# Four heads of the first input: three hardware-queue loads become five, one head each

## The chip, the cores and the metric

The kernel runs on one core of a Trainium2 chip. The metric is the device time of one execution in microseconds (us); lower is better. Times are given as the median of several executions; one further execution is recorded by the hardware profiler, and all lines of the profile come from that one.

A core has five engines that run at the same time, each with its own instruction queue: TensorE (PE, matrix products; PEld is its loading of weights), VectorE (DVE), ScalarE (ACT), GpSimd (POOL) and SyncE (SP). They wait for one another through semaphores only. Data between the main memory and the core's memory is moved by 16 DMA engines. A transfer is issued from the instruction queue of SyncE, ScalarE or POOL, and its packets then appear in the profile under that issuer's DMA queue: q1 for SyncE, q10 for ScalarE, q0 for POOL.

## The reference: what is computed

Cross attention between a long input x (8 batches, 8 heads, 512 rows, 64 columns) and a short state (32 rows), in both directions, and then a gated feed-forward layer on all 4352 rows of the result:

```python
scores = scale * np.matmul(x, state.transpose(0, 1, 3, 2))
a = np.exp(scores - scores.max(-1, keepdims=True))
xread = np.matmul(a / a.sum(-1, keepdims=True), state)
scores2 = scale * np.matmul(state, x.transpose(0, 1, 3, 2))
a2 = np.exp(scores2 - scores2.max(-1, keepdims=True))
sread = np.matmul(a2 / a2.sum(-1, keepdims=True), x)
y = concatenate([xread, sread], axis=2), heads side by side: (4352, 512)
out = (np.maximum(y @ w_gate, 0.0) * (y @ w_val)) @ w_out
```

w_gate and w_val are 512 x 1536, w_out is 1536 x 512; inputs and output are float32.

## The kernel before

Everything is computed in bf16 with float32 sums. For each batch the state's rows are multiplied with the gate and value weights first (U, in PSUM as `up` or `upc`), so that the gate and value of the long rows are one product of the normalised attention weights (`ans`) with U (`gv_ps`, line 325). ReLU runs on ScalarE (line 354), the product with the value on VectorE (line 358), the product with w_out on TensorE (`o_ps`, line 367), and the result leaves through SyncE's queue (line 379).

The order of every engine's instructions is written out by hand: the schedule is manual (line 412), and a program string (lines 455 to 483) lists the steps of the first two batches and part of the third in the order in which they are issued. A step is a name with numbers, and `@` gives the PSUM banks. Each engine takes its own instructions strictly in that order and waits where the data is not there yet. From line 525 on, loops issue the rest with fixed positions.

The steps that matter here are those of the first microseconds, for batch 0:

- Lines 414 to 420 load the state of batches 0 and 1 (`st_f`, 128 KB, `state_dma`, line 99) and heads 0 to 3 of batch 0 (`xf`, float32, 128 KB a head). SyncE issues heads 0 and 1 as one transfer, ScalarE the state and then heads 2 and 3 as one transfer. ScalarE then runs a one-element exp (line 421), which loads its table.
- Line 427 loads heads 4 to 7 of batch 0 from POOL, with the cast to bf16 on the way (`xb`). POOL goes on with batch 1 (`dx`, line 434) and then the weights (`dw`, line 109), in pieces.
- `spin32.2` and `spin` (line 440) are TensorE fillers whose result (`warm_ps`) is not used. The first fills TensorE until the state is there.
- `stc.0` casts the state on VectorE (line 118), `stT.0` transposes it on TensorE (line 123), `sto.0.0` and `sto.0.1` copy it out, on ScalarE and VectorE (line 140).
- `xc.0.0` casts heads 0 and 1 to bf16 on ScalarE, `xc.0.1` heads 2 and 3 on VectorE (both line 144).
- `xT.0.0.4` and `xT.0.4.4` transpose these pairs on TensorE (line 162), `xo` copies the transposes out (line 165): the first on VectorE, the second on ScalarE.
- `sc.0.0` computes the scores of heads 0 to 3 (line 179), `ex` their exp on ScalarE (line 206), `nr` the sums on VectorE (lines 212, 214), `nx` the scaling (line 218), and `aT`/`ao` transpose the weights into `ans`. Steps of batch 0's other heads and of batch 1 are woven in. The first `c` steps make U (line 298), and `gv.0.0` is the first product of the dense part.

The program's words around the change, of which TensorE, VectorE and ScalarE each take their own:

```python
xc.0.0.act spin.1.256 xT.0.0.4@1 xc.0.1.dve sto.0.0.act
spin.1.128 xT.0.4.4@2 xo.0.0.4.dve sto.0.1.dve xo.0.4.4.act spin.1 sc.0.0@3 ex.0.0 nr.0.0 spin.1.384
    xT.0.8.4@4 xT.0.12.4@5 xo.0.8.4.act xo.0.12.4.act spin.1 xT.1.0.8@6 sc.0.1@1 ex.0.1 xo.1.0.8.dve spin.1
```

So VectorE's queue holds, in this order, the cast of heads 2 and 3, the copy of the first transposes, and the copy of half the state; the scores wait for all of them.

Of the kernel before, what the change touches and what calls it, by code (L numbers as in the profile page):

```python
# [16 lines left out]
def kernel(  # L17
# [9 lines left out]
    nc = tc.nc  # L27
# [6 lines left out]
    NC = S // 128  # L34
# [43 lines left out]
    xf, xb, xT, eT, e_sn, a_sn, ANS, U, hsb = {}, {}, {}, {}, {}, {}, {}, {}, {}  # L78
# [18 lines left out]
    def state_dma(eng, lo, hi):  # L97
        src = state.rearrange("(g b) h (m i) d -> (b h m) g i d", b=2, i=4)
        eng.dma_start(out=st_f[:, lo // 2:hi // 2], in_=src[:, lo // 2:hi // 2])
# [312 lines left out]
    ctx.enter_context(tc.manual_schedule())  # L412
    nc.vector.memset(stT, 0.0)
    xf[0] = xin.tile([128, HK, NC, D], FP32, name="xf", tag="xf")
    for eng, j in ((nc.sync, 0), (nc.scalar, None), (nc.scalar, 1)):
        if j is None:
            state_dma(eng, 0, 2)
        else:
            src = x[0, 2 * j:2 * j + 2].rearrange("h (p c) d -> p h c d", c=NC)
            eng.dma_start(out=xf[0][:, 2 * j:2 * j + 2], in_=src)  # L420
    nc.scalar.activation(out=tiny, in_=nc.const_aps.tensor(0.0, (128, 1), FP32), func=AF.Exp)

    def w_load(w, lo, n):
# [179 lines left out]
```

## Time and profile before

| What | Value |
|---|---|
| Median of 3 executions | 220.07 us (219.66 to 220.4) |
| The profiled execution | 219.39 us |
| Its span, first to last instruction | 217.6 us |
| Issue to landing: state, ScalarE's queue, 128 KB | 2.6 us |
| Issue to landing: heads 0 and 1, SyncE's queue, 256 KB | 3.3 us |
| Issue to landing: heads 2 and 3, ScalarE's queue, 256 KB | 3.5 us |
| Issue to landing: heads 4 to 7 and batch 1's halves, POOL's queue, 256 KB each | 5.3 us (median of 3) |
| Granted TensorE clock | 1.00 in all slices |

The span is what the engines' instructions cover; the 1.8 us between it and the profiled execution's time lie around them. In lines of the timeline the first number is the start in us from the span's start, the second the length; then come the engine, the line of the kernel, the operation, what it writes and reads, and in brackets the idle time before it and what ended it. An engine name with a q (SPq, ACTq) is the issue of a transfer on that engine's queue. In the chain of waits a line is a piece of the chain that ended last: start, length, engine, tile and line.

### The profile page before, as it was taken

The page shows a single profiled execution, that of the slowest core. Times are in us where ns is not written, and L with a number is a line of the kernel's source. Part 1 is how long each engine was busy: PE and PEld are TensorE (multiplying, and loading weights), DVE is VectorE, ACT ScalarE, POOL GpSimd, SP SyncE. Part 2 cuts the span into 40 slices and gives each one's busy share as a digit, 9 for nine tenths or more (in the row PEclk, how much of TensorE's full clock was granted, in tenths as well). Part 3 has the DMA queues.
Part 4 walks back from the last instruction along what each step waited for, and adds up shares of the span by engine and source line. Part 5 has one row for each costly group of instructions (what it writes and reads, how often), then busy time and mean ns, then how long its engine had stood idle before and what let it go on. Part 6 is the DMA issues. An engine that isn't in the chain of part 4 may idle for free.

```text
span 217.6 us, 4865 instructions
## 1 busy us (share of the span) xinstructions
PE 212.8 (98%) x1952; PEld 104.8 (48%) x1952; DVE 135.0 (62%) x233; ACT 117.8 (54%) x225; POOL 42.5 (20%) x63
## 2 busy tenths in 40 slices
PE   8899999999999999999999999999999999999994
PEld 4554454454444444444444444444544445666543
DVE  4799967956887678557966796388745444222100
ACT  4798877747546556455555656454646443333221
POOL 7974049005600531020107000000000000000000
PEclk9999999999999999999999999999999999999999
DMA  7999999579963995919491453131311122222132
GB/s 168 180 196 197 202 221 171 78 139 188 152 175 74 144 186 110 167 52 193 99 148 60 110 134 96 49 99 50 84 28 51 48 48 50 61 56 80 51 96 96
DMA packets 47399, 24.96 MB, mean 115 GB/s; under 512 B 27824, under 2 KB 43056, under 8 KB 47376
## 3 DMA queue, kind: packets, MB, share of 16 engines
q0 software_dynamic: 16896, 9.05, 31.0%
q1 hardware_dynamic: 29584, 14.85, 28.7%
q10 hardware_dynamic: 896, 0.75, 1.3%
q8 instruction: 15, 0.25, 0.4%
q14 instruction: 8, 0.07, 0.2%
HBM read 18.35 MB, written 8.91 MB: 125 GB/s over the span
## 4 chain that ended last, share of the span: by engine, by line
PE 96%; DVE 1%; ACT 1%; issue 0%
PE o_ps L367 40%; PE gv_ps L325 38%; PE gv_ps L347 5%; PE up L298 4%; PE warm_ps L440 2%; PE upc L298 2%; PE o_ps L396 1%; PE sr_ps L265 1%; PE sc_ps L179 1%; PE sT_ps L189 1%; PE xT_ps L162 1%; ACT e_sn L206 1%; DVE xT L165 1%; ACT xT L165 0%; PE aT_ps L234 0%; DVE cs L212 0%
## 5 line engine op out<-in xcount | busy, mean ns | idle before, releaser
L367 PE MATMUL o_ps<-wo_sb,h_sb 128*128 128x512 bf16 x372 | 94.3, 379 | 0.0
L325 PE MATMUL gv_ps<-ans,U 128*128 128x512 bf16 x384 | 93.2, 379 | 0.0
L358 DVE TENSOR_TENSOR h_sb<-gv_ps,g_sb 128x512 bf16<-128x512 f32 x96 | 65.1, 688 | 42.8 <-ACT g_sb L354 41.3
L354 ACT ACTIVATE g_sb<-gv_ps 128x512 bf16<-128x512 f32 (+1 forms) x108 | 61.7, 578 | 51.4 <-PE gv_ps L325 39.1
L325 PEld LDWEIGHTS <-U 128*128 128x128 bf16 x384 | 37.1, 98 | 44.5 <-issue 0.8
L367 PEld LDWEIGHTS <-h_sb 128*128 128x128 bf16 x372 | 35.2, 98 | 42.0 <-issue 4.0
L310 DVE CAST U<-up 128x512 bf16<-128x512 f32 x44 | 27.7, 684 | 5.7 <-PE up L298 5.7
L375 ACT COPY o_sb<-o_ps 128x512 f32<-128x512 f32 x31 | 18.4, 594 | 19.7 <-PE o_ps L367 17.7
L310 ACT CAST U<-up 128x512 bf16<-128x512 f32 x28 | 14.7, 595 | 8.8 <-PE up L298 8.8
L254 POOL COPY xa<-xb 128x1024 bf16<-128x1024 bf16 x16 | 16.0, 1045 | 10.0 <-PE sr_ps L265 5.9
L358 DVE TENSOR_TENSOR hs_sb<-gv_ps,g_sb 128x256 bf16<-128x256 f32 x12 | 5.1, 425 | 15.3 <-PE gv_ps L347 10.4
L212 DVE TENSOR_REDUCE cs<-e_sn 128x16 f32<-128x512 bf16 x16 | 10.8, 677 | 1.1 <-ACT e_sn L206 1.1
L218 DVE TENSOR_TENSOR a_sn<-e_sn,rc 128x512 bf16<-128x512 bf16 x16 | 10.9, 687 | 0.4
L298 PEld LDWEIGHTS <-stT 64*32 64x32 bf16 x560 | 6.7, 91 | 6.4 <-issue 5.3
L320 ACT CAST U<-upc 128x512 bf16<-128x512 f32 (+1 forms) x19 | 8.7, 522 | 1.7 <-PE upc L298 1.7
L446 POOL COPY mark<-g_sb 128x1 bf16<-128x1 bf16 x4 | 0.8, 190 | 41.8 <-ACT g_sb L354 41.8
L197 ACT ACTIVATE eT<-sT_ps 128x512 bf16<-128x512 f32 x10 | 5.4, 594 | 5.3 <-PE sT_ps L189 5.3
L434 POOL DMA_DIRECT2D xb<-in_x_dram x8 | 6.8, 847 | 3.1 <-DMA wg_sb<-in_moe_w_gate_dram 1.4
L347 PE MATMUL gv_ps<-br,wg_sb 128*128 128x256 bf16 x48 | 7.2, 273 | 0.0
L347 PE MATMUL gv_ps<-br,wv_sb 128*128 128x256 bf16 x48 | 7.2, 273 | 0.0
L399 DVE COPY o_sb<-o_ps 128x64 f32<-128x64 f32 x2 | 0.4, 224 | 10.6 <-PE o_ps L396 10.5
L298 PE MATMUL up<-wg_sb,stT 64*32 64x512 bf16 (+1 forms) x168 | 6.9, 348 | 0.0
(59 smaller groups left out, 124.1 us busy)
## 6 DMA issues: line engine op xcount, KB each, us to landing
out_dram<-o_sb SPq DMA_DIRECT2D x26, 256.0 KB, 2.4
xb<-in_x_dram POOLq DMA_DIRECT2D x6, 512.0 KB, 7.1
wo_sb<-in_moe_w_out_dram POOLq DMA_DIRECT2D x2, 768.0 KB, 10.5
out_dram<-o_sb SPq DMA_DIRECT2D x11, 128.0 KB, 2.4
wg_sb<-in_moe_w_gate_dram POOLq DMA_DIRECT2D x5, 256.0 KB, 9.4
wv_sb<-in_moe_w_val_dram POOLq DMA_DIRECT2D x5, 256.0 KB, 10.0
xb<-in_x_dram POOLq DMA_DIRECT2D x3, 256.0 KB, 5.3
st_f<-in_state_dram POOLq DMA_DIRECT2D x1, 384.0 KB, 11.4
```

The source lines that it names most:

```text
L212: nc.vector.reduce_sum(out=cs, in_=e_v, axis=AX.X)
L218: {"dve": nc.vector, "pool": nc.gpsimd}[eng].tensor_tensor(out=a_sn[b][:, jp].rearrange("p c (j n) -> p c j n", n=Ns), in0=e_v, in1=held[" ...
L254: nc.gpsimd.tensor_copy(out=v[:, hs], in_=xb[b][:, hs])
L298: nc.tensor.matmul(dst[kc][i0:i0 + 32], stT[r:r + 64, parity, b, h], wsb[r:r + 64, j, lo:lo + n], start=True, stop=True)
L310: copy[eng](out=U[b][:, w, kc, lo:lo + 512], in_=held["u", b, w, lo][kc])
L320: copy[eng](out=U[b][:, :, kc, lo:lo + n], in_=held["c", b, lo][kc])
L325: nc.tensor.matmul(ps[w], U[b][:, w, kc, f0:f0 + 128], ANS[b][:, kc].rearrange("p c t -> p (c t)"), start=(kc == 0), stop=(kc == NK - 1))
L347: nc.tensor.matmul(ps[w][:, 0:nt], wsb[:, j, f0:f0 + 128], br[:, j].rearrange("p b n -> p (b n)"), start=(j == 0), stop=(j == NJ - 1))
L354: nc.scalar.activation(out=g_sb[:, 0:n], in_=ps[0][:, 0:n], func=AF.Relu)
L358: nc.vector.tensor_tensor(out=dst, in0=ps[1][:, 0:n], in1=held["g", b, jf][:, 0:n], op=ALU.mult)
L367: nc.tensor.matmul(held["o", b, tsub], src[:, jf, tsub * 128:(tsub + 1) * 128], wo_sb[:, jf], start=(jf == 0), stop=(jf == NF - 1))
L375: copy[eng](out=o_sb, in_=held["o", b, tsub])
```

## The change

Heads 0 to 3 of batch 0 are loaded with one transfer per head, not one per pair. SyncE issues heads 0, 1 and 3, in this order; ScalarE issues the state and then head 2. The same bytes go to the same places, and no other line differs. The cast of heads 0 and 1 now reads what two transfers of SyncE's queue wrote; the cast of heads 2 and 3 reads what one transfer of each queue wrote.

```diff
     nc.vector.memset(stT, 0.0)
     xf[0] = xin.tile([128, HK, NC, D], FP32, name="xf", tag="xf")
-    for eng, j in ((nc.sync, 0), (nc.scalar, None), (nc.scalar, 1)):
-        if j is None:
+    for eng, h in ((nc.sync, 0), (nc.scalar, None), (nc.sync, 1), (nc.scalar, 2), (nc.sync, 3)):
+        if h is None:
             state_dma(eng, 0, 2)
         else:
-            src = x[0, 2 * j:2 * j + 2].rearrange("h (p c) d -> p h c d", c=NC)
-            eng.dma_start(out=xf[0][:, 2 * j:2 * j + 2], in_=src)
+            eng.dma_start(out=xf[0][:, h], in_=x[0, h].rearrange("(p c) d -> p c d", c=NC))
     nc.scalar.activation(out=tiny, in_=nc.const_aps.tensor(0.0, (128, 1), FP32), func=AF.Exp)
```

## The prediction, made before the changed kernel ran

> **What bounds it.** I read the page's busy times and chain first, then the chain of waits in order of time for the first 14 us, then the timeline of those microseconds, then the DMA view in narrow stretches. Page, busy times and chain by engine:
>
> ```profile
> PE 212.8 (98%) x1952; PEld 104.8 (48%) x1952; DVE 135.0 (62%) x233; ACT 117.8 (54%) x225; POOL 42.5 (20%) x63
> ...
> PE 96%; DVE 1%; ACT 1%; issue 0%
> ```
>
> TensorE is the bound for the whole span. The change touches loads of the first 5 us alone, so it can only move the moment at which TensorE begins its dense work (13.07 us, the first gv_ps matmuls); whatever that moment moves, the end moves. The chain of waits there (start, length, what):
>
> ```profile
> 0.78 3.75 PE warm_ps L440 x4
> 4.53 0.43 PE stT_ps L123 x4
> 4.95 0.21 PE warm_ps L440
> 5.17 0.44 PE xT_ps L162 x4
> ...
> 5.63 0.42 DVE xT L165
> ...
> 6.09 0.44 DVE stT L140
> ...
> 6.57 0.44 PE sc_ps L179 x8
> ```
>
> No load stands in it: TensorE goes from its warm-up straight through state transposes, a filler and the transposes of heads 0 and 1; then two VectorE copies release the first scores. From 6.57 to 13.07 scores, exp, sums and copies follow each other with gaps of 0.02 to 0.05 us, so a delay of the scores is not won back. Now the loads and their users in the timeline:
>
> ```profile
> 0.73 0.43 ACTq L99 DMA_DIRECT2D st_f<-in_state_dram  x1
> 0.74 0.46 SPq L420 DMA_DIRECT2D xf<-in_x_dram  x1
> 1.19 0.45 ACTq L420 DMA_DIRECT2D xf<-in_x_dram  x1
> 1.25 0.89 POOL L427 DMA_DIRECT2D xb<-in_x_dram  x1 [0.81 <-POOLq L587]
> ...
> 4.01 0.62 ACT L144 CAST xb<-xf 128x512 bf16<-128x512 f32 x1 [0.84 <-DMA xf<-in_x_dram]
> ...
> 4.72 0.45 DVE L144 CAST xb<-xf 128x512 bf16<-128x512 f32 x1 [0.88 <-DMA xf<-in_x_dram]
> 4.75 0.57 PEld L162 LDWEIGHTS <-xb 128*128 128x128 bf16 x4
> ```
>
> Heads 0 and 1 land at 4.01 and are cast by 4.63; their weight loads begin at 4.75 and may begin as late as 4.86 (first transpose at 4.96, 0.10 per load). With 0.05 for the semaphore, the slack is 0.18 us. Heads 2 and 3 are cast by 5.17 and wanted at 5.39 (second group of weight loads): slack again 0.17. On VectorE the cast of heads 2 and 3 stands ahead of the copy at 5.63, with 0.46 idle between.
>
> **In what order the engines take the transfers.** Packets of single DMA queues in stretches: q10 is ScalarE's, q1 SyncE's, q0 POOL's (packets, MB, share of 16 engines). First line 2.9 to 3.2 us, second 3.6 to 3.88, third 4.3 to 5.2; the last two are from 109.40 on, SyncE's timeline and then the queue of 109.4 to 112.2:
>
> ```profile
> q1 hardware_dynamic: 114, 0.12, 108.5%
> ...
> q10 hardware_dynamic: 103, 0.11, 105.7%
> ...
> q0 software_dynamic: 328, 0.17, 141.3%
> ...
> 109.40 0.33 SPq L379 DMA_DIRECT2D out_dram<-o_sb  x1
> ...
> q0 software_dynamic: 820, 0.42, 119.7%
> ```
>
> The 16 engines are full from about 2.6 us and take whole transfers, one after the other: state, heads 0-1 (q1), heads 2-3 (q10), POOL's heads 4-7 (q0). POOL's transfer was probably ready before its turn: four later loads from line 434 moved their first packet 1.58 to 1.63 us after issue, so 1.25 + 1.6 = 2.85, yet q0 has no packet before 3.88. And a transfer once begun is not broken into: SyncE's store of 109.40 (stores into idle engines start after 0.84 us, so ready at 110.24) has no packet before 112.2, when POOL's 512 KB was through. The rows do not show how an engine chooses when several queues wait: by arrival, or by queue in turn.
>
> **The change, part by part.** The three transfers become five, each new one 128 packets of 1 KB, like the state's. Issues: SyncE does three instead of one, at about 0.74, 1.20 and 1.65 (0.43 for the state's issue of the same size, plus 0.03); SyncE's next work is at 43.90, so nothing queues behind them. ScalarE keeps two, its table load at 1.68 stays. POOL's queue is not touched, but it is passed: its transfer is now rivalled by one that is issued later than it, head 3 at 1.65. Two more completion packets per engine at 9 ns: 0.02 us, nothing. The ScalarE cast now waits for two transfers of SyncE, the VectorE cast for one of each queue; the extra wait is hidden in the 0.84 and 0.88 us that both sit idle, bounds 0 and 0.05 (the gap behind a semaphore in the chain).
>
> What can be gained: nothing. If heads 0 and 1 land earlier, their transposes still stand behind the filler at 4.95.
>
> What can be lost hangs on the order. Rates: q10 alone moved 103 packets in 0.28 us, 368 per us, so 128 packets take 0.35; q0 alone moved 328 in 0.90, so the 512 packets of POOL's 256 KB take 1.40.
>
> Case A, queues in turn. Each engine takes state (q10), head 0 (q1), head 2 (q10). That is the 24 KB per engine that state and heads 0-1 were before, ended at 3.20 to 3.60 by the completions. Next in turn is q0, ready since 2.85: 1.40, to 4.60 to 5.00. Then head 1: 0.35, to 5.35; the cast starts 0.42 after the last packet (4.01 - 3.59), at 5.77, ends 6.39. Then q0 again (the next load, issued 2.67, ready 4.27): 1.40, to 6.75; head 3: 0.35, to 7.10. VectorE's cast 0.44 later (4.72 - 4.28): 7.54 to 7.99. Late next: the copy of 5.63 goes to 8.03, that of 6.09 to 8.49, ending 8.92; scores at 8.97, not 6.57: +2.4. The transposes of heads 2-3 run 8.05 to 8.5 and ScalarE's copy to 9.1, so the scores' second half starts 9.15 and ends 9.5, not 7.01: +2.5. Sum: 219.39 + 2.5 = 221.9 for the profiled execution.
>
> Case B, by arrival, but head 3 comes behind POOL. Head 3 is ready 0.84 to 1.06 after its issue (the later stores; the state's first packet at 1.79): 2.49 to 2.71, against 2.85. A margin of 0.14 to 0.36 is what a slower third issue could eat. State, heads 0, 2, 1 end at 3.95, POOL 5.35, head 3 at 5.70, cast 6.14 to 6.59, copies to 7.52, scores 7.57 and second half later by 0.1: +1.1, 220.5.
>
> Case C, by arrival, POOL last. Heads 2-3 land where they did (40 KB per engine either way). Heads 0-1: head 2 is issued at 1.19, head 1 at 1.20; if head 2 goes first, head 1 is 0.35 late, less 0.18 slack: +0.17; else 0. Sum 219.39 to 219.6.
>
> I take A as the forecast. The bounds of the unknown price are 0 and +2.5.
>
> The Trainium skill, "DMA: Bandwidth & Descriptors", section "Queues, rings and completion order", says that each DMA engine goes round the queue rows that have work and drains a packet of up to 64 descriptors before it switches. By that rule the sum would be A's 221.9, and a pure order of arrival would give C's 219.4 to 219.6; the trace agrees that a transfer is not broken into (112.2 against 110.24), and leaves the going round open.
>
> **Rivals.** C is the other side, not slower: its place is the choice each engine makes at 3.20 to 3.60 us, its price +0.0 to +0.17, and it decides if POOL's descriptors count as later than heads 1 and 3. For it: POOL's transfer was ready about 2.85 and did not pass q10's pair at 3.2. Against it: that pair was also next in turn, and in the tail of the kernel four small stores of SyncE and ScalarE, issued alternately at 207.31 to 207.74, leave alternately, which fits both. B speaks for itself through its margin; against it, head 3 is ready first by each estimate. A fourth, D: A's gap stops TensorE, and it falls back to the rate of its start. Its first transposes took 0.43 for 4 (108 ns), later ones 0.45 for 8 (56 ns), though the granted clock reads 1.00 in all stretches; it left the slow rate about 4.7 us after its first matmul. If the gap brings it back at the first gv_ps matmuls, up to 4.7/2 = 2.35 us come on top of A: 224.3. Against it: the fillers stay in the program. E, faster: if TensorE left the slow rate before its transposes, the 1.08 us of 4.53 to 5.61 would take half, -0.54, and the state transposes, whose data is cast at 3.85, could start up to 0.47 before 4.32 were the warm-up shorter: 219.39 - 1.0 = 218.4. Nothing in the change brings either; the chance stands for what I have missed.
>
> **Chances.** A 0.36, B 0.16, C 0.32, D 0.06, E 0.10. The measured median before is 220.07 and its profiled execution 219.39, so 0.68 is added for a median: A 222.5 (rounded down from 222.6), B 221.2, C 220.1 to 220.3, D 225. A's own range is 221.8 to 223.2. With C's low end and run spread (219.66 to 220.4 before) the range is 219.7 to 223.8, leaving out most of D and E. 0.3% (0.66 us) is about what a measurement of this kernel can tell from no change: slower is A + B + D = 0.58, same is C = 0.32, faster E = 0.10.
>
> **What would show it.** Right: q0 has packets between 3.2 and 4.6 us, ahead of q1's last; the ScalarE cast at 5.8, VectorE's at 7.5, scores near 9, first gv_ps matmuls near 15.5, and the distance from there to the end unchanged. Wrong: casts at 4.0 to 4.4 and 4.7, q0 silent until 3.9 (C), or only VectorE's cast late, at 6.1 (B). If the casts are late but the gv_ps matmuls begin at 13.1, the chain of 6.57 to 13.07 had slack that I have denied.

## The result, and the profile after

| | Before | After |
|---|---|---|
| Median, 15 executions each, us | 219.87 (219.18 to 220.4) | 220.48 (219.73 to 221.4) |
| Ratio, with its 95% interval | | 1.0032 [1.0016, 1.0048] |
| Profiled execution and its span, us | 219.39; 217.6 | 221.32; 219.5 |

The change costs 0.3%, or 0.6 us, where 2.4 us were forecast. The executions of the changed kernel form two groups: ten at 219.73 to 220.63 with a mean granted clock of 0.998 to 1.0, and five at 221.31 to 221.4, four of them with a clock of 0.990 to 0.992. The profiled one is of the upper group, so its extra 1.9 us of span are not those of the median. (Without the `src` line all lines behind the loads are one lower than before: the loads are line 419, POOL's first load 426, the fillers 439.)

The timeline of the changed kernel (start, length, engine, line, operation; in brackets the idle time and what ended it):

```profile
0.74 1.35 SPq L419 DMA_DIRECT2D xf<-in_x_dram  x3
1.18 0.46 ACTq L419 DMA_DIRECT2D xf<-in_x_dram  x1
1.25 0.89 POOL L426 DMA_DIRECT2D xb<-in_x_dram  x1 [0.81 <-POOLq L586]
...
4.14 0.62 ACT L144 CAST xb<-xf 128x512 bf16<-128x512 f32 x1 [0.97 <-DMA xf<-in_x_dram]
...
6.20 0.45 DVE L144 CAST xb<-xf 128x512 bf16<-128x512 f32 x1 [2.34 <-DMA xf<-in_x_dram]
...
6.71 0.40 PE L162 MATMUL xT_ps<-id,xb 128*128 128x128 bf16 x4 [1.44 <-DVE xb L144]
...
7.49 0.69 PE L179 MATMUL sc_ps<-stT,xT 128*128 128x64 bf16 x8 [0.17 <-DVE stT L140]
```

ScalarE's cast of heads 0 and 1 is 0.13 later than before, VectorE's of heads 2 and 3 is 1.48 later (6.20 for 4.72), and the scores begin 0.92 later (7.49 for 6.57). The chain of waits of the same kernel now goes through the third load, where before no load stood in it:

```profile
1.19 0.42 SPq L419
...
1.66 4.45 DMA xf<-in_x_dram
...
6.20 0.45 DVE xb L144
6.65 0.33 DVE xT L165
...
7.01 0.44 DVE stT L140
...
7.49 0.69 PE sc_ps L179 x8
```

The same execution by stretches (us, busy time and instructions of PE, PEld, DVE, ACT, POOL, then the granted clock, the DMA share and GB/s):

```profile
6.00:8.00 2.00, 1.12 (x14) 0.75 (x15) 1.21 (x3) 0.58 (x1) 2.00 (x4) 0.90 1.35 167
8.00:10.00 2.00, 2.00 (x19) 1.56 (x17) 0.94 (x2) 1.64 (x3) 1.37 (x2) 0.50 1.52 170
10.00:13.00 3.00, 2.64 (x48) 1.92 (x47) 2.26 (x5) 1.77 (x4) 2.49 (x4) 0.83 1.71 184
```

The column to read is the clock: 0.50 at 8 to 10 us, 1.00 in every such stretch before. The first dense product starts at 15.02 instead of 13.01: 0.92 of these 2.01 are there at the scores, the rest is added behind them. Part of that rest does not need the low clock: a kernel below (e4) has its scores at the same 7.49, a full clock, and the product at 14.22. From that product to the end it is 204.5 us, as before (204.6).

The DMA queues between 3.6 and 4.6 us, first the changed kernel, then the one before (packets, MB, share of 16 engines):

```profile
DMA packets 189, 0.13 MB, mean 132 GB/s; under 512 B 14, under 2 KB 189, under 8 KB 189
...
q1 hardware_dynamic: 93, 0.08, 40.9%
q0 software_dynamic: 92, 0.05, 37.5%
q10 hardware_dynamic: 4, 0.00, 0.7%
```

```profile
DMA packets 381, 0.27 MB, mean 272 GB/s; under 512 B 16, under 2 KB 381, under 8 KB 381
...
q0 software_dynamic: 199, 0.10, 79.8%
q10 hardware_dynamic: 182, 0.17, 48.6%
```

In the changed kernel both queues are open in this microsecond, packets of both pass, and yet the engines move half of what they moved before. Among q1's packets are three of 1.1 to 1.4 us; before, none of the hardware queues' packets after 3 us took over 0.05. Each transfer closes with 16 packets of 4 bytes, read here as one for each of the 16 engines (the records do not name the engine). Those of head 3 lie at 3.86 to 5.80 us, the eleventh of them at 4.57: a few engines are late, and the cast waits for the last.

### The profile page after: what moved, and what is told of

It reads as the page before. It is cut to its first block, busy times and chain, and to the rows that moved or that the text cites. A ratio compares the mean times of both kernels' runs of the same rounds, so it can differ in the third digit from the quotient of the medians.

```text
span 219.5 us, 4845 instructions
## 1 busy us (share of the span) xinstructions
PE 210.5 (96%) x1926; PEld 105.2 (48%) x1952; DVE 134.9 (61%) x233; ACT 117.8 (54%) x225; POOL 42.5 (19%) x63
## 4 chain that ended last, share of the span: by engine, by line
PE 93%; DMA 2%; issue 2%; DVE 1%; ACT 1%; SPq 0%; DVEq 0%
PE o_ps L367 38%; PE gv_ps L325 38%; PE gv_ps L347 5%; PE up L298 4%; DMA xf<-in_x_dram 2%; PE upc L298 2%; PE o_ps L396 1%; PE xT_ps L162 1%; PE sr_ps L265 1%; PE sc_ps L179 1%; PE sT_ps L189 1%; DVE xT L165 0%; ACT xT L165 0%; PE aT_ps L234 0%; SPq L419 0%
## 5 line engine op out<-in xcount | busy, mean ns | idle before, releaser
L367 PE MATMUL o_ps<-wo_sb,h_sb 128*128 128x512 bf16 x354 | 90.6, 379 | 2.4 <-issue 2.2
```

What stands on the lines that cost most here:

```text
L367: nc.tensor.matmul(held["o", b, tsub], src[:, jf, tsub * 128:(tsub + 1) * 128], wo_sb[:, jf], start=(jf == 0), stop=(jf == NF - 1))
```

## The experiments

The table has what every later paragraph reads; all but the ratio is taken from the one profiled execution of each kernel. "Last" is the hardware transfer that lands last and its place in its queue; "closing packets" are the first, the eleventh and the last of its 16; "cast" is the later of the two casts. POOL's issue is that of its first load.

| Kernel | Last | Its issue ends | POOL's issue ends | Closing packets | Cast | Scores | Ratio |
|---|---|---|---|---|---|---|---|
| before | 2nd | 1.64 | 2.14 | 3.88, 4.21, 4.28 | 4.72 | 6.57 | 1 |
| after | 3rd | 2.09 | 2.14 | 3.86, 4.57, 5.80 | 6.20 | 7.49 | 1.0032 [1.0016, 1.0048] |
| e1_pool_later | 3rd | 2.09 | 2.34 | 3.71, 4.91, 5.52 | 5.92 | 7.19 | 1.0029 [1.0013, 1.0046] |
| e2_split01 | 2nd | 1.64 | 2.14 | 3.81, 4.03, 4.12 | 4.55 | 6.05 | 0.9995 [0.9983, 1.0008] |
| e3_split23 | 2nd | 1.71 | 2.14 | 3.87, 4.17, 4.27 | 4.81 | 6.44 | 0.9989 [0.9975, 1.0003] |
| e4_fill | 3rd | 2.09 | 2.14 | 3.85, 5.19, 5.73 | 6.12 | 7.49 | 1.0037 [1.002, 1.0053] |
| e5_h3_scalar | 3rd | 2.12 | 2.14 | 4.15, 5.05, 6.13 | 6.58 | 7.85 | 1.0078 [1.0052, 1.0103] |
| e6_h1_third | 3rd | 2.08 | 2.15 | 3.77, 4.87, 5.17 | 5.59 | 7.84 | 1.0082 [1.0051, 1.0113] |
| e7_pool_much_later | 3rd | 2.08 | 3.37 | 3.56, 4.04, 4.38 | 4.79 | 6.54 | one execution |
| e8_three_of_four | 3rd | 2.18 | 2.14 | 4.97, 5.20, 6.78 | 7.20 | 8.47 | 1.0089 [1.0061, 1.0118] |
| e9_second_late | 2nd | 1.71 | 2.14 | 3.92, 4.19, 4.27 | 4.81 | 6.31 | 0.9987 [0.9974, 1.0] |
| e10_fill_long | 3rd | 2.18 | 2.14 | 4.88, 5.11, 5.64 | 6.14 | 7.92 | 1.007 [1.0048, 1.0092] |
| e11_second_later | 2nd | 2.29 | 2.14 | 5.19, 5.37, 5.49 | 5.99 | 7.50 | 1.0095 [1.006, 1.013] |
| e12_three_pool_later | 3rd | 2.18 | 3.37 | 3.88, 4.23, 4.35 | 4.83 | 6.57 | one execution |
| e13_second_209 | 2nd | 2.09 | 2.14 | 4.14, 4.46, 4.77 | 5.34 | 6.75 | 1.0005 [0.9984, 1.0027] |
| e14_second_189 | 2nd | 1.90 | 2.14 | 4.24, 4.41, 4.56 | 5.16 | 6.75 | 0.9998 [0.998, 1.0015] |
| e15_third_lead | 3rd | 2.09 | 2.62 | 3.74, 4.08, 4.19 | 4.71 | 6.57 | 1.0061 [1.0037, 1.0085] |
| e16_four_lead | 3rd | 2.18 | 2.33 | 3.85, 5.50, 5.69 | 6.10 | 7.37 | 1.0045 [1.0023, 1.0067] |

### POOL's first load a little later

```diff
-    nc.gpsimd.dma_start(out=xb[0][:, HK:H], in_=x[0, HK:H].rearrange("h (p c) d -> p h c d", c=NC))
     make_identity(nc, id128)
+    nc.gpsimd.dma_start(out=xb[0][:, HK:H], in_=x[0, HK:H].rearrange("h (p c) d -> p h c d", c=NC))
```

> The changed kernel with POOL's two first steps exchanged: its load of heads 4 to 7 is issued after the identity matrix is made, about 0.6 us later (near 1.85 us instead of 1.25). Theory S (POOL's transfer shares the engines with head 3, packet by packet, and that makes head 3 late): head 3 has the engines for itself until about 4.2 us, VectorE's cast of heads 2 and 3 starts at 4.7 to 5.2 us instead of 6.20, and the time is that of the kernel before to 0.1 us. Rival R (head 3 is late through its own third issue on SyncE and slow reads, POOL or not): the cast stays at 5.6 us or later and the time at +0.4 to +0.7 us.

POOL's issue moved by 0.2 us only, too little to take its packets out of the way: its first packet came at 3.63 us, as in the changed kernel. Head 3 was late as before, and the run decides nothing between the two theories.

### Each pair split alone

The first kernel splits heads 0 and 1 only, the second heads 2 and 3 only (`lo` to `hi` are the heads, `None` the state; only the loop's first line is shown, its body loads `lo` to `hi` in one transfer):

```diff
+    for eng, lo, hi in ((nc.sync, 0, 1), (nc.scalar, None, 0), (nc.sync, 1, 2), (nc.scalar, 2, 4)):
```

```diff
+    for eng, lo, hi in ((nc.sync, 0, 2), (nc.scalar, None, 0), (nc.scalar, 2, 3), (nc.sync, 3, 4)):
```

> Only heads 0 and 1 are split (two transfers of SyncE); heads 2 and 3 stay one transfer of ScalarE behind the state. Both theories: nothing is issued third, so heads 2 and 3 land near 4.7 us, heads 0 and 1 near 4.1 us; within 0.2 us of the kernel before. If splitting itself cost the time, by more packets or more issues, half of the loss (+0.3 us) would be seen here.

> Only heads 2 and 3 are split: SyncE heads 0 and 1 as one transfer, then head 3, which is now its second issue (about 1.23 us instead of 1.66); ScalarE the state and head 2. Theory S: head 3's descriptors are there some 0.4 us earlier, ahead of POOL's; VectorE's cast at 4.7 to 5.2 us, the time within 0.2 us of the kernel before. Rival R (the split of the pair over two queues is what is slow): the cast at 5.6 us or later and +0.4 to +0.7 us.

Neither loses anything, though each has four transfers, two per queue, in place of three. So it is not the smaller transfers, nor a cast that waits for two of them, that costs the time.

The first also shows where an earlier start goes. In the kernel with heads 0 and 1 split the scores begin 0.52 us earlier than before, the first dense product 0.21 later. The loads did not bring the scores forward, since TensorE had not waited for them before either. In this execution TensorE had left the slow rate of its start ahead of the transposes of heads 0 and 1 (first the kernel before, then this one):

```profile
4.96 0.63 PE L162 MATMUL xT_ps<-id,xb 128*128 128x128 bf16 x4
...
4.69 0.39 PE L162 MATMUL xT_ps<-id,xb 128*128 128x128 bf16 x4
```

When that happens differs from one profiled execution to the next, whatever the loads: these four transposes took 0.63 us in e1 too, and 0.40 in the changed kernel. So scores in the table that differ by up to 0.5 us need not differ through the loads. Between two executions at the fast rate, this one and the changed kernel's, the scores are 1.44 us apart (6.05 and 7.49), about the 1.48 of the late cast; against the kernel before it was 0.92. The timeline of TensorE goes on:

```profile
6.05 0.54 PE L179 MATMUL sc_ps<-stT,xT 128*128 128x64 bf16 x8 [0.22 <-DVE stT L140]
...
11.22 0.25 PE L298 MATMUL upc<-wv_sb,stT 64*32 64x128 bf16 x8 [0.49 <-DMA wv_sb<-in_moe_w_val_dram]
...
13.22 1.04 PE L325 MATMUL gv_ps<-ans,U 128*128 128x512 bf16 x3
```

The wait in the second line is for POOL's first value weights. That is a second path of nearly the same length, and an earlier start of the scores ends there.

### The gap in TensorE filled

```diff
-    spin.1.128 xT.0.4.4@2
+    spin.4 xT.0.4.4@2
```

> The changed kernel with TensorE's filler between the transposes of heads 0-1 and of heads 2-3 lengthened from one matmul of 128 columns to four of 512 (about 0.9 us at the full rate), inside the gap of 5.2 to 6.7 us. Theory C (the gap makes TensorE's granted clock fall to a half at 8 to 10 us in some executions): the clock reads 1.00, the gv_ps matmuls begin near 14.0 us, and no execution lies 0.9 us above the others as five of fifteen did; median +0.4 to +0.5 us. If the fall has another cause, the upper group of executions near 221.3 us stays.

The median did not fall (220.63), but the clock stayed at 0.998 to 1.0 in all 12 executions. Two of the 12, at 221.19 and 221.84, were slow all the same. At full clock the scores began as late as in the changed kernel and the first dense product at 14.22. The chain of waits of that kernel shows why the fill saves little: the second path is late too.

```profile
4.17 0.71 POOL wg_sb L109
4.89 7.11 DMA wv_sb<-in_moe_w_val_dram
```

The value weights are there at 12.00, in the kernel with heads 0 and 1 split at 11.19 (4.89 + 6.30). POOL's own stream has lost time in the microsecond in which the engines ran at half rate (83 packets of q0 there, 127 in the split kernel).

### Another queue, another head

```diff
-    for eng, h in ((nc.sync, 0), (nc.scalar, None), (nc.sync, 1), (nc.scalar, 2), (nc.sync, 3)):
+    for eng, h in ((nc.sync, 0), (nc.scalar, None), (nc.sync, 1), (nc.scalar, 2), (nc.scalar, 3)):
```

```diff
-    for eng, h in ((nc.sync, 0), (nc.scalar, None), (nc.sync, 1), (nc.scalar, 2), (nc.sync, 3)):
+    for eng, h in ((nc.sync, 0), (nc.scalar, None), (nc.sync, 3), (nc.scalar, 2), (nc.sync, 1)):
```

> The changed kernel with head 3 issued by ScalarE as its third transfer (state, head 2, head 3); SyncE heads 0 and 1. Theory R (the third transfer issued in a row on a hardware queue is served slowly, whichever queue): VectorE's cast still at 5.7 us or later, +0.4 to +0.7 us. Theory Q (it is SyncE's queue): cast at 5.2 us or earlier, within 0.2 us of before.

> The changed kernel with heads 1 and 3 exchanged on SyncE (0, 3, 1). Theory R: now head 1 is the late one, so ScalarE's cast of heads 0 and 1 starts at 5.5 us or later and VectorE's cast of heads 2 and 3 at 4.2 to 4.8 us. If head 3's place in memory is what is slow: ScalarE's cast at 4.0 to 4.2, VectorE's late as in the changed kernel.

With head 3 third on ScalarE's queue it is just as late, and with head 1 third it is head 1, so that ScalarE's cast waits (5.59) and VectorE's does not (4.42). Neither SyncE's queue nor head 3's data is the cause; it is the transfer that is issued third on its queue that comes late.

### POOL's packets taken away

```diff
     xb_alloc(0)
+    nc.gpsimd.memset(spare[:, 0:2048], 0.0)
     nc.gpsimd.dma_start(out=xb[0][:, HK:H], in_=x[0, HK:H].rearrange("h (p c) d -> p h c d", c=NC))
```

> The changed kernel with a fill of unused memory on POOL before its first load, so that POOL's transfers of heads 4 to 7, of batch 1 and of the weights all begin some 2 us later; its time is not to be compared. Theory S (POOL's packets make head 3 late): with no q0 packet before 5 us, VectorE's cast starts at 4.7 to 5.0 us. Theory R: head 3's packets are slow all by themselves, cast at 5.3 us or later.

> Three of four transfers on SyncE's queue, and POOL's first load held back by a memset of 1.8 us, so that none of its packets moves before about 4 us. The sum of the time is not comparable, since all of POOL's work is later; what is read is when head 3, third on SyncE's queue, lands. Theory S (a third transfer loses only by sharing the engines with POOL's packets): head 3 lands by 4.4 and VectorE's cast starts by 4.9. Rival H (a third transfer is held back for itself, until the first of its queue is complete, 3.24 to 3.74 in that kernel, plus some 0.85 us): the engines run empty about 4.0, head 3's packets come from 4.1 to 4.6 on, and the cast starts at 5.2 or later even without POOL.

The first is the changed kernel, the second the kernel of the next paragraph, each with that line. The sums (221.25 and 222.91) have POOL's later chain in them. What is read is the cast, here of the first:

```profile
4.79 0.43 DVE L144 CAST xb<-xf 128x512 bf16<-128x512 f32 x1 [0.85 <-DMA xf<-in_x_dram]
```

POOL's first packets come at 4.09 and 4.13 us here, when most of the third transfer is through (closing packets from 3.56 and 3.88 on). With hardly a packet of POOL beside it a third transfer lands in time in both kernels. It is not held back by its place alone.

### Three of four on one queue, and the fill again

```diff
+    for eng, lo, hi in ((nc.sync, 0, 2), (nc.scalar, None, 0), (nc.sync, 2, 3), (nc.sync, 3, 4)):
```

The second run (e10) is this kernel with a longer fill:

```diff
-    spin.1.128 xT.0.4.4@2
+    spin.11 xT.0.4.4@2
```

> Four transfers in all, but three of them on SyncE: heads 0-1 together, head 2, head 3; ScalarE the state alone. Theory R (third in a row on its queue): VectorE's cast at 5.5 us or later, +0.3 to +0.7 us. Theory F (it is the fifth transfer in flight, on any queue): cast at 4.7 to 5.0 us, within 0.2 us of before.

> Three of four transfers on SyncE's queue as before (VectorE's cast 7.2, the largest loss, 1.0089), but TensorE's idle time of 2.1 us ahead of the transposes of heads 2-3 is filled with 11 products of 512 columns in place of one of 128. Theory D (the idle time makes the granted clock fall to 0.5 to 0.7 at 8 to 13 us in most executions, and that costs some 1 us of the loss): casts late as before, about 7, but the granted clock 1.00 in all slices, mean clock 1.0 in nearly all executions, and the ratio falls to 1.003 to 1.006. Rival (the clock reading is a by-product and all of the loss is the late cast): ratio 1.007 to 1.011 whatever the clock reads. If the filler only runs into the transposes, scores at 8.5 to 9 as before.

A fifth transfer is not needed for the loss. Here the third's issue ends 0.04 after POOL's, and all 16 engines take it late (first closing packet at 4.97, against 3.86 in the changed kernel). The stretches of the kernel without and then with the long fill:

```profile
8.00:10.00 2.00, 1.81 (x19) 1.33 (x17) 0.60 (x2) 1.24 (x3) 1.42 (x2) 0.66 1.53 169
10.00:13.00 3.00, 2.93 (x37) 2.26 (x35) 2.12 (x5) 1.77 (x4) 2.29 (x4) 0.66 1.71 183
```

```profile
8.00:10.00 2.00, 1.66 (x27) 1.29 (x26) 0.50 (x1) 1.62 (x4) 1.45 (x3) 1.00 1.70 182
10.00:13.00 3.00, 2.21 (x44) 1.34 (x43) 2.87 (x7) 2.33 (x4) 2.97 (x5) 1.00 1.64 188
```

Eight of ten executions without the fill had a mean clock of 0.991 or 0.992, none of six with it (0.999 and 1.0). With the short fill above (none of 12, against four of 15) this shows that TensorE's idle time brings the low clock on. What the clock costs this run does not price: the ratio fell only to 1.007, which is what was expected if the clock cost nothing, but the cast was earlier too (6.14 for 7.20), and the fill itself ran to 7.64 us while the cast was done at 6.66, so the scores (7.92) waited for the fill. In the profiled executions with the scores at 7.49 or 7.50 the low clock goes with 0.80 us: the first dense product is at 14.22 in e4, with the full clock, and at 15.02 in the changed kernel and in e11, with the low one. The other executions do not bear out a fixed price: the slowest of e5 (222.49) and of e11 (223.21) had a mean clock of 1.0.

### Place in the queue, or time of issue

```diff
-    nc.vector.memset(stT, 0.0)
     xf[0] = xin.tile([128, HK, NC, D], FP32, name="xf", tag="xf")
+    nc.vector.memset(xf[0][:, 3], 0.0)
+    nc.vector.memset(stT, 0.0)
```

This stands in the kernel with heads 2 and 3 split (e3), where head 3 is second on SyncE's queue; its issue waits for the memset of its place. There is one such memset in e9, three in e11, two in e14, and in e13 two and one of a quarter of the place.

> The kernel with heads 0-1 as a pair and head 3 on SyncE, the state and head 2 on ScalarE (two transfers on each queue, no loss so far), but head 3's issue is held back to about 1.6 us, where the changed kernel issues it, by a VectorE memset of 0.25 us into its place, put ahead of the 1.76 us memset that VectorE starts with. Theory T (the third transfer in a row on a queue is late, because it is third): head 3 is only second here and lands in time; VectorE's cast at 4.7 to 5.0, scores at 6.4 to 6.7, ratio 0.998 to 1.001. Rival I (what counts is only the time of its issue, 1.65 us, about when POOL has finished issuing its own): VectorE's cast at 5.9 to 6.6, scores at 7.2 to 7.9, ratio 1.002 to 1.006.

> As the run before (SyncE: heads 0-1, head 3; ScalarE: state, head 2), whose one memset was over at 1.13 us and so held nothing back; now three of them, 0.27 us each from 0.86 on, so that head 3's issue, second on SyncE's queue, begins at 1.6 to 1.7 us. Theory T (late because third in a row on its queue): VectorE's cast at 4.7 to 5.1, scores 6.4 to 6.8, ratio 0.998 to 1.002. Rival I (late because issued at 1.65, about when POOL finishes its own issue): VectorE's cast 5.9 to 6.6, scores 7.2 to 7.9, ratio 1.002 to 1.006.

> SyncE: heads 0-1, head 3; ScalarE: state, head 2. Head 3 is second on its queue, and its issue is held back by VectorE memsets (two of 256 elements, one of 64) so that it ends at about 2.1 us, as the third issue of the changed kernel does (2.09), 0.05 ahead of the end of POOL's issue (2.14). Theory I (what decides is how long a hardware issue ends before POOL's, whatever its place in its queue): VectorE's cast at 5.7 to 6.6 as in the changed kernel (6.20), ratio 1.002 to 1.008. Theory T (its place, third, decides, and the run with three memsets was late only because it ended 0.15 after POOL's): cast at 4.7 to 5.1, ratio 0.998 to 1.002.

> The same with two memsets of 256 elements: head 3's issue, second on SyncE's queue, ends at about 1.9 us, 0.25 ahead of POOL's. In the run with the identity moved, a third transfer with a lead of 0.25 was late (cast 5.92). Theory I: a second transfer with this lead is late too, cast 5.5 to 6.2, ratio 1.001 to 1.006, or, if the bound lies between, on time in some executions and late in others. Theory T: cast 4.7 to 5.0, ratio 0.998 to 1.001.

One memset (e9) held nothing back, so that run is a repeat of e3. Three of them moved the issue's end to 2.29, past POOL's, and head 3 was late on all engines: issued after POOL's, a transfer is late whatever its place. It does not stand behind the whole of POOL's transfer, though. At 4.6 to 5.2 us packets of both pass side by side, and head 3's last closing packet (5.49) is ahead of the first of POOL's (5.69):

```profile
q0 software_dynamic: 104, 0.05, 64.0%
q1 hardware_dynamic: 99, 0.10, 60.1%
```

But a second transfer issued at the third's time (2.09), or at 1.90, was not torn apart: casts at 5.34 and 5.16, later than 4.81 but ahead of the 5.9 to 6.6 of VectorE's cast where the third was torn apart, and no loss in time. Neither cast lies in the range of either theory. The DMA queues at 3.6 to 4.6 us with the issue at 2.09:

```profile
DMA packets 412, 0.33 MB, mean 334 GB/s; under 512 B 39, under 2 KB 412, under 8 KB 412
...
q1 hardware_dynamic: 193, 0.17, 50.8%
q0 software_dynamic: 93, 0.05, 34.8%
q10 hardware_dynamic: 126, 0.11, 32.5%
```

That is the full rate, against 189 packets in the changed kernel, with POOL's packets among them too. The pure theory of issue time falls with this run. In both kernels the memsets also made the state's cast late (3.95 and 3.66 for 3.42 in e3), and ScalarE's cast of heads 0 and 1 waited for its loads until 4.54 and 4.31, for 4.00 in e3. That is as much as VectorE's cast is later (0.53 and 0.35 us), so 5.34 and 5.16 are not head 3's lateness alone.

### The third with a longer lead, and a third of four

The first is the changed kernel with a shorter memset ahead of POOL's load, the second e8 with the identity made ahead of it, as in e1:

```diff
     xb_alloc(0)
+    nc.gpsimd.memset(spare[:, 0:1152], 0.0)
     nc.gpsimd.dma_start(out=xb[0][:, HK:H], in_=x[0, HK:H].rearrange("h (p c) d -> p h c d", c=NC))
```

> The changed kernel with POOL's first load held back by a memset of some 1 us (1152 elements of a scratch tile), so that its issue begins at about 1.75 and ends at about 2.65, and head 3's, third on SyncE's queue, at 2.09: a lead of 0.55, somewhat more than the 0.43 with which a second transfer was in time. Theory I: the lead decides, so head 3 lands in time although it is third: VectorE's cast 4.7 to 5.0, scores 6.5 to 6.7. Theory T (third place, with POOL's packets coming before head 3 is through): cast later than 5.4. The sum also has POOL's later chain in it (about +0.5), so it is the casts that are read.

> Four transfers, three of them on SyncE's queue (heads 0-1, head 2, head 3; ScalarE: the state), with POOL's identity made ahead of its first load, so that POOL's issue ends at about 2.34 and head 3's at 2.18. So far, of five transfers, the third whose issue ended 0.02 to 0.25 ahead of POOL's came late on some of the 16 engines, with packets of 0.5 to 1.4 us and half the rate at 3.6 to 4.6 us; a second with a lead of 0.05 or 0.24 did not; and in the two kernels with four transfers and a third, the third's issue ended after POOL's. Theory T (third place): head 3 late on some engines, VectorE's cast 5.5 to 6.6, ratio 1.002 to 1.007. Rival F (five transfers of 128 KB, not the third place; and behind POOL only if issued after it): head 3 lands on all engines within 0.8 us, no packet over 0.45 us, VectorE's cast 4.7 to 5.4, ratio 0.998 to 1.002.

With 0.53 us between the ends of the two issues the third lands in time (4.71); the loss in the sum (1.0061) then comes from POOL's later chain: from the first dense product to the end it is 205.6 us, for 204.5. With a lead of 0.15 and only four transfers it is late again, at 6.10. Its 16 closing packets (us) are in two lots, eight engines in time and eight more than a microsecond behind:

```
3.85 3.86 3.90 3.91 3.91 4.16 4.17 4.19 | 5.27 5.46 5.50 5.52 5.56 5.58 5.66 5.69
```

It has packets of 0.5 to 1.4 us on q1, and at 3.6 to 4.6 us 141 packets in all, 36 of them POOL's. So a third place on a queue is enough for the half rate at such a lead, and a fifth transfer is not needed.

## Why the prediction failed, step by step

**The sign was right, the size was not.** Forecast was case A at +2.4, the median went up by 0.6, and the likeliest case was not the one that happened. The range held the result because it reached down to case C; its upper end, 223.8, is not worked out from the cases.

**The step that failed is the order of the engines.** "Take whole transfers, one after the other" and "a transfer once begun is not broken into" were read from rows in which one queue had the engines almost to itself. With two hardware queues open they alternate within a transfer. The kernel before shows it already, at 2.1 to 2.9 us, where the state and heads 0 and 1 pass together (first two lines), and the changed kernel at 2.4 to 2.9 us with the state and head 0 (last two):

```profile
q10 hardware_dynamic: 91, 0.08, 35.5%
q1 hardware_dynamic: 82, 0.08, 34.0%
...
q1 hardware_dynamic: 102, 0.09, 52.1%
q10 hardware_dynamic: 101, 0.09, 51.7%
```

In the changed kernel the closing packets of the two run in pairs 0.09 us apart, from 2.42 and 2.51 to 2.85 and 2.94. POOL's 256 KB never stood ahead of head 1 for 1.40 us: head 1's last closing packet lies at 3.71, POOL's first packet at 3.63. ScalarE's cast moved by 0.13 and not by 1.76, and case A falls. The Trainium skill, "DMA: Bandwidth & Descriptors", section "Queues, rings and completion order", says that an engine goes round its queues packet by packet. The trace agrees if the profile's packets of 1 KB are the packets meant (102 against 101); if they are descriptors, of which that section counts about 9 to 17 in a packet, the trace shows a finer turn than it states. The prediction had made a whole transfer of that packet, and that gave the 221.9. Alternation does not explain all rows: the store of 109.40 had no packet before 112.2 beside a load of POOL's that was issued earlier, much as in e8 and e11 a transfer issued after POOL's comes late, and why stays open.

**What happened looks like case B, by another way.** Its sign, only VectorE's cast late, at 6.1, is what the profile shows (6.20), and its +1.0 at the scores is near the measured 0.92. Its reason holds in part in the runs whose issue ended after POOL's (e8 and e11): head 3 then starts late, but passes beside POOL's packets and not behind the last of them. In the changed kernel head 3's issue ends 0.05 ahead of POOL's and eleven engines are through by 4.57; the last five make the loss. B put the whole transfer behind POOL at 5.70, close to the last packet at 5.80, but for a reason that does not hold here, so the nearness is luck. Its margin, "what a slower third issue could eat", was the right place to look, and the 0.43 per issue was right (1.35 for three).

**"A delay of the scores is not won back"** held in the profiled execution: the 0.92 at the scores had grown to 2.01 at the first dense product, and 1.93 of these reached the end. Over many executions the median rose by 0.56 among those without a low clock (median 220.43 of eleven), less than 0.92. The path of POOL's weights, which took over in e2, e4 and e9, would explain that, but the kernel before was profiled once, without that wait, so this is argued and not shown.

**Case D, given 0.06, had a real mechanism.** It was priced on top of A's gap, which did not come, but TensorE waited 1.44 us and the clock fell to 0.50. Four of 15 executions carry that mark. They lie in the group at 221.3, 0.9 above the other, with a fifth that does not carry it; the case had allowed up to 2.35. What spoke against it, that the fillers stay, was wrong: the one ahead of the wait ends at 5.27, 1.44 us too early, and those behind the waiting transposes in TensorE's order wait with them.

**Case E, given 0.10, met half its condition and not its time.** In the execution of the kernel with heads 0 and 1 split TensorE had left the slow rate before those transposes, and the scores were 0.52 earlier, near the 0.54 of the case; the state transposes did not move forward. The time did not fall, since the first dense product then waited for POOL's value weights, a path that the prediction had not listed.

**Case C's price was right where it applies.** With two transfers per queue the split cost nothing (0.9995 and 0.9989). The steps costed at nothing, the second wait of each cast and the extra closing packets, are confirmed there. No version tried is shown to be faster than the kernel before: the best, e3 and e9, read 0.9989 and 0.9987 with intervals that reach 1.0.

## What to carry to other kernels

Before splitting a load, see when its last piece will be issued against the next queue's traffic: each further issue on one engine costs 0.45 us. Here two pieces per queue cost nothing, while a third made its cast 1.2 to 1.9 us late when the issue of POOL's transfer ended up to 0.25 us after its own, and came in time at 0.53 us. Look at all closing packets of a transfer, since the last of the 16 sets the wait, and spread pieces over queues before stacking them on one. A wait of TensorE can be followed by a low clock, so it is worth filling; but a filler works only ahead of the waiting instruction in TensorE's order, and its length has to fit the wait: too short, it leaves the gap (the changed kernel), too long, it becomes the delay itself (e10).

## What the runs showed of the hardware that was not expected

- The two regimes of the third transfer. Issued after POOL's load (e8, e10, with e11 as a second) its first closing packet came at 4.88 to 5.19 us. Issued 0.02 to 0.25 us ahead (after, e1, e4, e5, e6, e16) its first came at 3.71 to 4.15 and its last at 5.17 to 6.13, with packets of 0.6 to 1.4 us on the hardware queues. From 3 us on, no hardware packet of the other kernels took over 0.38 us.
- The engines are not full meanwhile: 141 to 243 packets in the microsecond from 3.6 us in these six kernels, 274 in e2 and 353 to 418 in the other kernels with at most two transfers per queue. The count alone does not mark the loss: e15, in time, has 261. Why a third transfer and POOL's slow each other down, when a second of the same issue time does not, stays open; the packet records do not name the engine.
- The granted clock fell after less idle time than thought. The Trainium skill, "TensorE: Matmul & The Clock Gate", section "What's actually happening", puts the fall behind an idle window of about 3.4 us; in the changed kernel TensorE was idle for 1.44 us in one piece, among shorter ones, and read 0.90 at 6 to 8 us and 0.50 at 8 to 10; in e11 the longest piece was 1.26 us, and five of six executions carry the low clock.
